# Paired dilated tails, slot sums from the exponentials and wide slot outputs in a windowed attention and soft-MoE kernel

## The chip, the cores and the metric

The kernel runs on one core of one Trainium2 chip. The time is the device time of a run in microseconds; a profile's span, from the first to the last instruction, is some 1.7 us shorter than the time of the same run. A run more than 1.5% above the fastest of its kernel is marked slow. Each group of experiments ran on one chip beside runs of the kernel before on the same chip; the groups used different chips.

Engines are named as in the profile: PE multiplies matrices, PEld loads its weights, DVE and ACT are the vector and scalar engines, POOL is GpSimd, which also issues nearly all transfers, and SP issues the last two. The clock is the share of full speed that PE was granted.

A timeline's line has the start and length in us, the engine, the line of the kernel, what is written and read, for PE the rows and columns of the array that a product uses (`64*128`: 64 rows), the operand's size, how many were merged, and in brackets the idle time before it with what ended it.

## The reference, cut to what matters

```python
def _attn_ref(q, k, v):                       # (8, 8, 576, 64): batch, heads, positions, width
    scores = matmul(q, k.T) / 8
    rel = pos[:, None] - pos[None, :]
    mask_plain = (rel >= 0) & (rel < 32)                       # heads 0 to 3
    mask_dil = (rel >= 0) & (rel < 128) & (rel % 4 == 0)       # heads 4 to 7
    return matmul(softmax(where(mask, scores, -1e9)), v)

def _moe_ref(x, phi, w1, w2):                 # x (4608, 512), 8 experts of 4 slots each
    logits = x @ phi                          # (4608, 32)
    d = softmax of logits over the rows       # slot sums: column sums of exp(logits)
    slot_input = d.T @ x
    slot_out[e] = relu(slot_input[e] @ w1[e]) @ w2[e]
    return softmax(logits over slots) @ slot_out
```

All inputs and the output are fp32 in HBM. The kernel computes in fp16, and the transfers cast.

## The kernel before

A dilated head of 576 positions is four interleaved subsequences of 144 positions: 128 and a tail of 16. In the kernel before each tail is a product of its own, for scores and for values. The attention of a batch and the work that follows it (transposes to x^T, logits, slot sums U) run in a software pipeline over eight batches.

```python
# scores of group 1: two plain tiles, then the four dilated tails
for r in range(DIL):
    w = LEFT if r < 3 else 2 * LEFT                                  # LEFT = 16
    jobs.append((kd, SUB * r + 96, qd, SUB * r + 128, W1 + LEFT * r, w))
...
# values of the tails, one product of 48 x 32 for each head and subsequence
for r in range(DIL):
    c0 = W1 + LEFT * r
    jobs.append((32 * r, 32, n, pt[0:48, h % 2, c0 : c0 + 32], vL[b % NV][0:48, h, r, 0 : D + 1]))
...
# slot sums: a product of ones beside the two products of x for every tile t
jobs.append((4, ones[0:n, :], er[0:n, t, :]))
...
# slot outputs, in two halves of 256 columns
slot_out(0, ORDER[:6]); slot_out(1, ORDER[:6]); slot_out(0, HALVED)   # HALVED = (6, 7)
for pair in range(NSPLIT // 2):
    combine(0, pair)                                                  # first outputs
    ...
```

The weights w2 of experts 6 and 7 arrive last, in two column halves: the first half of the output is computed and written while the second half of these weights is still on its way. The two last pairs of output tiles go out through SP; all other transfers are issued by POOL.

The softmax here doesn't subtract the row's maximum and nothing guards it: scores larger than these inputs give would overflow.

## Time and profile before

| | before |
|---|---|
| time, median of 4 runs | 182.15 us (182.03 to 182.48) |
| span and clock of the profiled run, a fifth one of 182.69 us | 181.0 us, 0.868 |
| PE, DVE, ACT, POOL busy | 81%, 59%, 50%, 46% of the span |
| read, written | 61.93 MB, 9.44 MB: 394 GB/s over the span |
| batch period at full clock (start of the same logits product, 97.32 to 110.99) | 13.67 us |
| first products with w1 | 138.87 us |
| first output issued | 152.88 us |

The batch period counts only where the clock is 1.0 throughout, which it was from 80 to 128 us.

### The profile page before, as it was taken

The numbers are of one execution on the slowest core, as the hardware profiler recorded it, in microseconds if no ns is written. First come the engines' busy times: TensorE is split into PE (matmuls) and PEld (weight loads), VectorE is DVE, ScalarE is ACT, GpSimd is POOL, SyncE is SP. The second block draws the span as 40 slices with busy tenths as digits, with TensorE's granted clock in tenths as the row PEclk, the third lists the DMA queues.
The fourth block names the chain that finished last, engine by engine and source line by source line (L and its number), as shares of the span: only waits on it lengthen the run. The fifth ranks groups of instructions, "written<-read, shape, count | busy, mean of one in ns | idle before, by whom it ended". The sixth has DMA issues, their size and how long they took to land.

```text
span 181.0 us, 5591 instructions
## 1 busy us (share of the span) xinstructions
PE 146.4 (81%) x2464; PEld 87.4 (48%) x2464; DVE 107.5 (59%) x232; ACT 91.0 (50%) x162; POOL 83.9 (46%) x124
## 2 busy tenths in 40 slices
PE   0467977999999999999999999999987986598000
PEld 0133544746755665664674674675735363233000
DVE  4689874875757676588498498453604023389030
ACT  2044454748465484755766776675430024488030
POOL 7953552642623263352544327434410442979900
PEclk9999995798589789789999999999855699879855
DMA  4999999999999999999999999999999999999996
GB/s 60 199 196 208 208 210 214 201 211 214 202 212 214 203 212 214 201 211 213 203 214 211 204 216 210 214 215 215 211 216 213 200 193 163 311 332 409 410 404 239
DMA packets 29527, 40.75 MB, mean 225 GB/s; under 512 B 1856, under 2 KB 19264, under 8 KB 29504
## 3 DMA queue, kind: packets, MB, share of 16 engines
q0 software_dynamic: 28960, 39.36, 116.3%
q1 hardware_dynamic: 544, 1.05, 1.5%
q8 instruction: 19, 0.31, 0.6%
q14 instruction: 4, 0.03, 0.0%
HBM read 61.93 MB, written 9.44 MB: 394 GB/s over the span
## 4 chain that ended last, share of the span: by engine, by line
DMA 43%; PE 34%; ACT 6%; DVE 6%; POOL 5%; issue 3%; POOLq 0%; DVEq 0%
DMA w<-in_moe_w_dram 28%; DMA raw<-in_k_dram 9%; ACT p L293 5%; PE lg L408 5%; PE o_p L339 4%; PE sa L282 4%; DMA out_dram<-ol 4%; PE sb L271 4%; PE sa L271 4%; DMA out_dram<-ot 2%; PE rd L389 2%; DVE qk L245 2%; PE vb L163 2%; PE va L163 2%; PE u L452 2%
## 5 line engine op out<-in xcount | busy, mean ns | idle before, releaser
L293 ACT ACTIVATE p<-sa 128x960 f16<-128x960 f32 (+2 forms) x24 | 21.4, 891 | 33.9 <-PE sb L282 33.4
L339 PEld LDWEIGHTS <-p 128*128 128x128 f16 (+2 forms) x544 | 19.7, 99 | 12.8 <-issue 8.6
L245 DVE STREAM_TRANSPOSE qk<-raw 128x320 uint32<-128x320 uint32 (+1 forms) x32 | 21.6, 678 | 0.3
L271 PE MATMUL sa<-masks,ident 128*128 128x480 f16 (+2 forms) x48 | 15.6, 414 | 7.3 <-POOL masks L489 6.2
L293 ACT ACTIVATE p<-sb 128x960 f16<-128x960 f32 (+2 forms) x24 | 21.2, 884 | 0.0
L236 DVE STREAM_TRANSPOSE qk<-raw 128x576 uint32<-128x576 uint32 x16 | 19.8, 1249 | 0.9 <-DMA raw<-in_q_dram 0.8
L271 PEld LDWEIGHTS <-ident 128*128 128x128 f16 x96 | 9.6, 112 | 18.9 <-issue 7.7
L282 PEld LDWEIGHTS <-qk 32*128 32x128 f16 x832 | 12.6, 100 | 12.0 <-issue 9.8
L408 PE MATMUL lg<-xTd,phi 128*128 128x288 f16 x32 | 18.3, 659 | 0.0
L339 PE MATMUL o_p<-v,p 128*128 128x65 f16 (+1 forms) x288 | 16.6, 202 | 0.8 <-ACT v L172 0.7
L282 PE MATMUL sa<-qk 32*128 32x160 f16 (+4 forms) x416 | 16.5, 217 | 0.8 <-DVE qk L236 0.7
L282 PE MATMUL sb<-qk 32*128 32x160 f16 (+4 forms) x416 | 16.5, 218 | 0.0
L271 PE MATMUL sb<-masks,ident 128*128 128x480 f16 (+2 forms) x48 | 15.4, 411 | 0.5 <-ACT p L293 0.5
L209 POOL COPY v<-v 32x1024 f16<-32x1024 f16 x8 | 8.3, 1036 | 16.1 <-PE sb L282 9.4
L212 POOL DMA_DIRECT2D w<-in_moe_w_dram x16 | 8.9, 554 | 14.4 <-DMA vs<-in_v_dram 6.8
L361 DVE TENSOR_TENSOR xp<-o_p,rc_p 128x448 f16<-128x448 f32 (+1 forms) x24 | 14.4, 602 | 0.8
L361 DVE TENSOR_TENSOR xd<-o_d,rc_d 128x448 f16<-128x448 f32 (+1 forms) x24 | 14.4, 602 | 0.8
L219 POOL DMA_DIRECT2D w<-in_moe_w_dram x10 | 6.7, 673 | 14.5 <-DMA w<-in_moe_w_dram 10.2
L163 PE MATMUL va<-vs,orders 32*128 32x256 f16 (+1 forms) x96 | 12.1, 289 | 1.0 <-ACT p L293 1.0
L412 ACT ACTIVATE ET<-lg 128x288 f16<-128x288 f32 x16 | 6.6, 411 | 12.3 <-PE lg L408 12.1
L360 DVE RECIPROCAL rc_p<-o_p 128x7 f32<-128x7 f32 (+1 forms) x24 | 4.8, 198 | 12.1 <-PE o_p L339 11.6
L382 ACT COPY xTp<-rp 128x576 f16<-128x576 f16 x16 | 10.4, 647 | 2.2 <-PE rp L377 2.2
(108 smaller groups left out, 277.9 us busy)
## 6 DMA issues: line engine op xcount, KB each, us to landing
w<-in_moe_w_dram POOLq DMA_DIRECT2D x16, 512.0 KB, 16.8
w<-in_moe_w_dram POOLq DMA_DIRECT2D x5, 1024.0 KB, 19.3
vs<-in_v_dram POOLq DMA_DIRECT2D x8, 512.0 KB, 14.5
raw<-in_q_dram POOLq DMA_DIRECT2D x7, 576.0 KB, 16.6
raw<-in_k_dram POOLq DMA_DIRECT2D x7, 576.0 KB, 16.8
out_dram<-ot POOLq DMA_DIRECT2D x14, 256.0 KB, 4.2
out_dram<-of POOLq DMA_DIRECT2D x7, 512.0 KB, 4.9
w<-in_moe_w_dram POOLq DMA_DIRECT2D x8, 256.0 KB, 10.2
```

The lines of the kernel that those rows point to most:

```text
L163: nc.tensor.matmul(o.rearrange("p (h d) -> p h d", h=4), l, st[:, 0:4, D * r : D * r + D], start=(r == 0), stop=(r == DIL - 1), skip_group ...
L209: nc.gpsimd.tensor_copy(out=vL[b % NV][0:32, :, :, 0:D], in_=vD[b % NV][96:128, :, :, 0:D])
L212: nc.gpsimd.dma_start(out=w1t[e][:, 2 * i : 2 * i + 2, :].rearrange("p l f -> p (l f)"), in_=moe_w1[e, 256 * i : 256 * i + 256].rearrange( ...
L236: nc.vector.transpose(out=dst, in_=src)
L245: nc.vector.transpose(out=o, in_=i)
L271: nc.tensor.matmul(sps[h // 2][:, h % 2, 0:n], ident, bias[g], start=True, stop=False, skip_group_check=True,)
L282: nc.tensor.matmul(sps[h // 2][:, h % 2, c0 : c0 + w], kt_[32 * h : 32 * h + 32, k0 : k0 + 128, tt], qt_[32 * h : 32 * h + 32, q0 : q0 + w ...
L293: nc.scalar.activation(out=pt, in_=sps[ab][:, :, 0:n], func=AF.Exp, scale=SCALE)
L339: nc.tensor.matmul(o[p0 : p0 + np_, n, :], l, rr, start=(k == 0), stop=(k == len(jobs) - 1), skip_group_check=True,)
L361: nc.vector.tensor_tensor(out=x.rearrange("p t (h d) -> p (t h) d", h=4)[0:nq, u0:u1, :], in0=o[0:nq, 0:n, 0:D], in1=rc[0:nq, 0:n, None].b ...
L382: nc.scalar.copy(out=xTp_t[b][:, c, :], in_=rg)
L408: nc.tensor.matmul(lp, phi4[:, kc].rearrange("p c s -> p (c s)"), rhs, start=(kc == 0), stop=(kc == 3))
```

## The change

Its intent is to take work off PE. The four dilated tails of a head are put in pairs: keys of all four subsequences are gathered into one tile kL by a DVE copy, two products of 64 columns replace four small ones, and the values become two products per head. The slot sums come from the accumulator of ACT's exponential, so the products of ones and the mask of the slot rows go away. The dilated tail's transposes and its products in U use 64 rows and stand next to each other, apart from the 128-row ones; the plain tail's products in U, of 64 rows before, take all 128. The first six experts' slot outputs are computed 512 columns wide, kept aside, and added to the halves of the last two experts on DVE.

```diff
 # scores, group 1
-                for r in range(DIL):
-                    w = LEFT if r < 3 else 2 * LEFT
-                    jobs.append((kd, SUB * r + 96, qd, SUB * r + 128, W1 + LEFT * r, w))
-                n = W1 + NLEFT                                       # 304
+                for u in range(2):
+                    jobs.append((kL[b % 2], 128 * u, None, 0, W1 + NLEFT * u, NLEFT))
+                n = W1 + 2 * NLEFT                                   # 352
...
+                    if qt_ is None:
+                        qq = qd[heads, 0:S, tt].rearrange("p (r i) -> p i r", r=DIL)[:, 128:SUB]
 # values of the tails
-                for r in range(DIL):
-                    ...                                              # 48 x 32, four to a head
+                for u in range(2):
+                    c1 = W1 + NLEFT * (u + 1)
+                    m = (128, 64)[u]
+                    (jobs, over)[u].append(
+                        (128 - m, m, n, pt[:, h % 2, c1 - m : c1], vL[b % NV][:, h, u, 0 : D + 1])
+                    )
 # transposes of the dilated part
-        for r in range(DIL + 1):
+        for r in (0, 1, 2, 3, 4) if c == 0 else (4, 0, 1, 2, 3):
+            p0 = 0 if r < DIL else NLEFT                             # NLEFT = 64
             nc.tensor.transpose(
-                rg[:, 128 * r : 128 * r + 128], xd_t[b][:, r, 128 * c : 128 * c + 128], ident
+                rg[:, 128 * r : 128 * r + 128 - p0],
+                xd_t[b][p0:128, r, 128 * c : 128 * c + 128],
+                ident[p0:128, p0:128],
             )
 # logits and slot sums
-        nc.scalar.activation(out=ET[:, c0 : c0 + n], in_=lp, func=AF.Exp, scale=1.0)
+        nc.scalar.activation(..., accum_out=esum[:, 2 * b + half : 2 * b + half + 1])
...
-            jobs.append((4, ones[0:n, :], er[0:n, t, :]))
 # prologue
+        nc.vector.tensor_scalar(out=masks[:, W1:], in0=masks[:, W1:], scalar1=gap, ..., op0=ALU.max)
 # slot outputs
-        slot_out(0, ORDER[:6])
-        slot_out(1, ORDER[:6])
-        slot_out(0, HALVED)
+        slot_out(so_early, 0, early, True, True)                     # six experts, 512 columns
+        nc.scalar.copy(out=early_sb, in_=so_early)
+        for n in range(2):
+            slot_late(0, n)                                          # then early_sb + so on DVE
```

Cut here: mask building for the pairs (nine selections on POOL instead of five), the layout of vL and kL, the four smaller POOL copies that fill vL, one transpose instead of four in the slot rows, and the small product that spreads the slot sums over the partitions at the end of attention.

## The prediction

> **What bounds the kernel now.** I read the page's rows over 40 slices first, because a kernel with several stages hides behind averages: the summary says PE 81% busy, and that is the wrong thing to believe.
>
> ```profile
> PE   0467977999999999999999999999987986598000
> ...
> DMA  4999999999999999999999999999999999999996
> GB/s 60 199 196 208 208 210 214 201 211 214 202 212 214 203 212 214 201 211 213 203 214 211 204 216 210 214 215 215 211 216 213 200 193 163 311 332 409 410 404 239
> ...
> HBM read 61.93 MB, written 9.44 MB: 394 GB/s over the span
> ```
>
> PE looks full over the middle, but the DMA row is full from the second slice to the last but one, and the moved bytes never fall below about 200 GB/s while inputs load. The loads cast fp32 to fp16, so 61.93 MB read arrive as 30.97 MB. Two stages follow: loads at about 210 GB/s as written (420 GB/s as read), then the output at about 409 GB/s. Estimate of the DMA work alone: 30.97 MB / 209 GB/s = 148 us, plus 9.44 MB / 409 GB/s = 23 us, plus 2.6 us before the first bytes, is 174 of the 181.0 us span.
>
> Next I read the chain that ended last, in order of time, to see whether PE's 15 us per batch or the queue carries the end.
>
> ```profile
> 86.15 16.32 DMA raw<-in_k_dram
> ...
> 102.77 21.17 DMA w<-in_moe_w_dram
> ...
> 125.33 19.26 DMA w<-in_moe_w_dram
> ...
> 146.34 10.34 DMA w<-in_moe_w_dram
> 156.72 0.32 PE so L722 x4
> 157.06 0.38 ACT so_sb L730
> 157.48 2.73 PE f L801 x6
> ```
>
> From 86 us on it is transfers end to end, except for short issues. A load of 512 KB takes 16.8 us from issue to landing (the page's DMA issues), though at 209 GB/s its bytes need 2.5 us: some 14 us of queue stand in front of it. Before 86 us the chain walks through PE because the k load was issued after a DVE transpose, but with 14 us queued a later issue does not leave the DMA engines empty: the bandwidth row shows no hole.
>
> Last the turn from loads to output, from the timeline of PE and the table of windows (columns: stretch, busy of PE, weight loads, DVE, ACT, POOL, clock, DMA share, GB/s).
>
> ```profile
> 138.87 5.82 PE L686 MATMUL hps<-w,siTm 128*32 128x512 f16 x64 [1.06 <-DVE siTm L672]
> ...
> 146.54 3.38 PE L722 MATMUL so<-w,hTm 128*32 128x256 f16 x104 [0.38 <-DVE hTm L703]
> 151.04 0.29 PE L722 MATMUL so<-w,hTm 128*32 128x256 f16 x4 [1.11 <-DMA w<-in_moe_w_dram]
> ```
> ```profile
> 148.00:152.00 4.00, 2.42 (x72) 1.91 (x63) 0.00 (x0) 0.37 (x1) 0.00 (x0) 1.00 1.44 194
> 152.00:154.00 2.00, 1.79 (x20) 1.00 (x18) 1.71 (x4) 1.82 (x5) 1.12 (x3) 1.00 0.83 116
> 154.00:156.00 2.00, 0.97 (x16) 0.50 (x9) 1.26 (x2) 1.06 (x3) 2.00 (x3) 1.00 1.37 254
> ...
> 160.00:162.00 2.00, 1.76 (x8) 0.78 (x7) 1.84 (x4) 1.88 (x5) 1.73 (x3) 0.90 1.03 258
> 162.00:178.00 16.00, 5.25 (x23) 2.11 (x22) 6.67 (x10) 6.13 (x13) 9.55 (x14) 0.77 1.60 407
> ```
>
> The last four slot products of the first half start at 151.04 after 1.11 us of waiting for the w2 load. All PE work before them was done at 149.9, so a faster PE gains nothing here; a slower one has 1.1 us to spare. Only two holes exist: 152 to 154 (116 instead of 194 GB/s, so 2 x (1 - 116/194) = 0.8 us) and 160 to 162 (258 instead of 407, so 0.73 us). Together 1.5 us: all that compute could give back.
>
> **What the skill says.** "DMA: Bandwidth & Descriptors", section Specifications, gives 435 GB/s as the fabric's ceiling and about 358 GB/s for HBM per core. The trace agrees with the first (2 x 212 = 424 as read) and not with the second (394 over the whole span, 409 written). The same page, section "Anatomy of one DMA — SWDGE (gpsimd) path", says that waits happen at the issuing sequencer and that the engines just consume their queues; the 14 us of queue fit. So later or earlier issues don't matter until that queue is drained. "TensorEngine Tiling", section Key Properties, says that changing the tiling mode drains TensorE. That is the change's reason for grouping 64-row products; no row of before separates that cost. "VectorE: DVE Perf Modes", section on the TRN2 errata, gives (N+151)/0.96 ns for an fp32 two-operand add: 424 ns for 256 elements. No 256-element add from PSUM is in this trace; its nearest row, the relu of 256 from PSUM, took 0.43 us.
>
> **The change part by part.** *Attention, per batch at full clock.* Scores of group 1: the mask product grows from 304 to 352 columns, four times; mean starts of 256- and 480-column products suggest 0.4 ns a column, so 4 x 48 x 0.42 = +0.08 us. Of the dilated tails 32 small products, starting over 0.2 us (119.28 to 119.49), become 16 of 64 columns; the eight of 64 columns at 119.22 start over 0.06 us, so 0.12: -0.1. Values: 16 products of 48 rows become 8; the 18 of the last chunk take 0.40 to 0.47 us, about 25 ns each, so 8 x 25 = -0.2. Slot rows: 13 transposes become 10, -0.08. Slot sums: 25 products become 20; 25 took 0.94 to 1.01 us, some 40 ns each with clock losses, so -0.2. PE: **-0.5 us a batch, about -4 us over eight**, before drains saved. ACT: exp of 704 instead of 608 elements, (891-677)/352 = 0.6 to 0.9 ns an element, 2 x 96 x 0.85 = +0.16 us; sums beside the 16 exps of the logits, about +0.1. DVE: the gather of 4 x 48 words about +0.25 us, the masked product of 320 (0.33 us) becomes a plain copy, -0.1. POOL: four copies of 512 elements instead of two of 1024 (1.03 us each), +0.1. All of it is beside the transfers.
>
> *Prologue.* POOL makes nine mask selections instead of five, at about 0.27 us (1.29 us for four): +1.1 us. The new DVE maximum over the masks stands ahead of the first q transpose (6.33 us) and waits for the last selection, at 6.75 + 1.1 = 7.85: the first transposes begin about 1.7 us later. But six loads have been issued by 5.1 us; their 1.73 MB keep the queue busy past 11 us at about 200 GB/s, and the next load moves only from 6.70 to 7.8. Cost to the end: 0.
>
> *Slot sums in the tail of attention.* Reduction, diagonal, one small product and the reciprocal replace one reciprocal (0.29 us): four short steps at 0.15 to 0.3 us, +0.5 to +0.8, partly beside 1.09 us of zero fills. Net for PE before the slot outputs: -4 + 1.7 + 0.6, so 1 to 2 us earlier, into the wait for w2. Gain 0.
>
> *Wide slot outputs.* 96 products of 256 columns become 48 of 512. The stream is the same (104 took 3.38 us, 32 ns each, four side by side); perhaps -0.4 us, again ahead of the wait at 151.04. On the path afterwards a DVE add (about 0.43) stands where an ACT cast (0.37) stood: +0.06 us for each half. The early copy of 512 columns lies in the wait.
>
> *Transfers.* No load or store changes its bytes, its shape or its order. Sum on the path: 0 + 0 + 0 + 0.06 + up to 0.06 = **+0.1 us**, and the PE time saved turns into a longer wait for w2.
>
> **The rivals.** *PE carries the end after all.* The row of nines and the chain before 86 us speak for it; then 4 us less PE would make about 178.5. Against it are the bandwidth row without a hole and PE's wait at 151.04. I give it 1 in 50. *The holes close.* If the clock is full at 158 (it was 0.50 in the window 158 to 160, where six wide products took 2.72 us), the first full-width outputs come 0.4 us earlier and time falls to 181.6; if the throttle lands on the slot outputs instead, 182.8. *The delay comes through.* If prologue and slot sums cost more than thought and PE saves nothing, the slot products end 2.5 us later, overrun the 1.1 us of slack by 1.4 and widen the hole at 152: 183.3 at most. *POOL contention:* smaller copies and waits on DVE delay load issues; harmless while 14 us are queued.
>
> **Range and chances.** Before has a median of 182.14 with runs from 182.03 to 182.48 (the profiled one 182.69), so 0.3% is noise. The prediction is the same time, 182.1 us: +0.1 from the path, and as much back from a PE that stays ahead. Eight in ten: 181.3 to 183.1, from the clock's luck in the holes below and the delay rival above. Faster by over 2% would need 178.5 or less, that is 3.6 us, when the holes hold 1.5: 0.02. Slower by over 2% (above 185.8) would need the queue to run dry during attention: 0.02. Within 2%: 0.96.
>
> **What would show each step.** Right: PE and weight-load busy time fall by several us; loads stay at 200 to 215 GB/s; the last w2 landing stays at 156 to 157; the wait of the slot products for w2 grows from 2.9 us in total. Wrong: a w2 landing that moves by more than 1 us, load bandwidth that differs, or a hole in the DMA row before 150. A later first transpose of about 8 us with no effect at the end would confirm the prologue step. The prediction fails if the queue's bandwidth depends on what the engines do beside it.

## The result, and the profile after

The changed kernel measured 182.41 us (four runs: 182.09, 182.33, 182.49 and a slow one of 184.93) beside 182.15 us before. The ratio is the mean time of one kernel's fast runs over that of the other's in the same rounds, so it is not quite the ratio of these medians: 1.0006, 95% interval 0.9985 to 1.0027.

The profile taken then fell on the slow run. The changed kernel was therefore run twice more (labels again and again_b below), and both of these profiles are of fast runs. The page of the first of them, PE's and the transfers' rows over 40 slices:

```profile
PE   0357886999999999999999999999997888776100
...
DMA  4999999999999999999999999999999999999995
GB/s 65 196 197 207 211 206 215 200 212 212 203 212 215 200 213 216 200 214 211 203 211 216 205 209 216 215 213 212 214 219 210 194 197 157 296 392 408 408 375 215
```

The transfers' row is again full from the second slice to the last but one, at the same 200 to 215 GB/s for the most part; the bytes are the same (61.93 MB read, 9.44 MB written). PE's row is as full as before although it has 2162 products instead of 2464. The slice from 149.6 us shows 157 GB/s where before had 163.

The chain that ended last, in order of time, has one new piece. (The columns are start, length, piece.)

```profile
124.46 19.44 DMA w<-in_moe_w_dram
...
145.64 0.74 POOL w L236
146.38 6.96 issue
153.36 0.53 POOL out_dram L796
```

Before, a transfer of 10.34 us and the last slot products stood in that place; here POOL has issued its last load and waits 6.96 us until the first output is there to be issued. The output comes from PE. So PE's timeline around the turn from loads to output tells more; lines of three profiles of the changed kernel, itself unaltered, follow, first the fast run of again:

```profile
140.95 5.72 PE L728 MATMUL hps<-w,siTm 128*32 128x512 f16 x64 [0.62 <-DVE siTm L714]
...
148.53 2.56 PE L768 MATMUL so_early<-w,hTm 128*32 128x512 f16 x44 [0.38 <-DVE hTm L745]
150.92 0.61 PE L768 MATMUL so<-w,hTm 128*32 128x256 f16 x16
```

then the fast run of again_b:

```profile
137.03 6.32 PE L728 MATMUL hps<-w,siTm 128*32 128x512 f16 x64 [0.62 <-DVE siTm L714]
...
149.62 0.29 PE L768 MATMUL so<-w,hTm 128*32 128x256 f16 x4 [1.05 <-DMA w<-in_moe_w_dram]
```

then the slow run:

```profile
142.51 6.03 PE L728 MATMUL hps<-w,siTm 128*32 128x512 f16 x64 [0.62 <-DVE siTm L714]
```

Before began the products with w1 at 138.87 and waited for w2. The changed kernel begins them at 137.03, 140.95 or 142.51, in three runs of the same program. In the first it waits 1.05 us for w2, as before did; in the second all 16 products of the first half follow each other without a wait, because PE is the later one. In the slow run, too, they follow each other without a wait, and end at 153.4.

What differs between these runs is the clock. Its mean from 12 to 80 us was 0.97 in again_b and 0.92 in again (0.85 before), and from 128 to 148 us 0.74 against 0.57 (0.66 before). The work per batch at full clock is the same in all: 14.12 us in again (82.11 to 96.23) and in again_b (79.82 to 93.94). So a batch became **0.45 us longer**, where the prediction had it 0.5 us shorter, and whether that reached the turn went with the clock. All 16 runs of the changed kernel divide by it: the eight with a clock of 0.902 or less took 182.74 to 184.93 us, the eight with 0.909 or more 181.78 to 182.72. The 33 runs of before beside the experiments, at 0.869 to 0.912, show no such division (181.51 to 183.16). Six of the first eight ran on one chip, and what sets the clock of a run is not shown, so this is two measured things going together and no proof of the cause.

### The profile page after: what moved, and what is told of

The parts are those of the page before. It is cut to its first block, busy times and chain, and to the rows that moved or that the text cites. A ratio compares the mean times of both kernels' runs of the same rounds, so it can differ in the third digit from the quotient of the medians.

```text
span 183.2 us, 5048 instructions
## 1 busy us (share of the span) xinstructions
PE 147.7 (81%) x2162; PEld 85.3 (47%) x2162; DVE 111.0 (61%) x253; ACT 93.2 (51%) x177; POOL 87.3 (48%) x144
## 3 DMA queue, kind: packets, MB, share of 16 engines
q1 hardware_dynamic: 544, 1.05, 1.5%
HBM read 61.93 MB, written 9.44 MB: 390 GB/s over the span
## 4 chain that ended last, share of the span: by engine, by line
DMA 36%; PE 34%; issue 10%; ACT 7%; POOL 6%; DVE 3%; POOLq 0%; DVEq 0%; ACTq 0%
DMA w<-in_moe_w_dram 22%; DMA raw<-in_k_dram 8%; PE sa L302 6%; PE o_p L354 5%; ACT p L313 5%; PE lg L426 5%; DMA out_dram<-ol 4%; PE sb L286 4%; PE sa L286 4%; DMA out_dram<-of 2%; PE rd L405 2%; PE vb L167 2%; PE va L167 2%; POOL out_dram L834 1%; POOL raw L142 1%
## 5 line engine op out<-in xcount | busy, mean ns | idle before, releaser
L313 ACT ACTIVATE p<-sa 128x960 f16<-128x960 f32 (+2 forms) x24 | 22.0, 917 | 36.2 <-PE sb L302 36.2
L354 PEld LDWEIGHTS <-p 128*128 128x128 f16 (+2 forms) x480 | 21.4, 103 | 14.0 <-issue 9.8
L313 ACT ACTIVATE p<-sb 128x960 f16<-128x960 f32 (+2 forms) x24 | 21.9, 912 | 0.0
L216 POOL COPY v<-v 32x512 f16<-32x512 f16 x16 | 9.7, 609 | 22.5 <-DVE v L206 22.0
L354 PE MATMUL o_p<-v,p 128*128 128x65 f16 (+1 forms) x288 | 17.1, 206 | 0.7 <-ACT v L176 0.7
L302 PEld LDWEIGHTS <-qk 32*128 32x128 f16 x576 | 10.5, 102 | 13.5 <-issue 10.0
L302 PE MATMUL sa<-qk 32*128 32x160 f16 (+2 forms) x288 | 14.7, 240 | 2.2 <-DVE qk L245 2.2
L302 PE MATMUL sb<-qk 32*128 32x160 f16 (+2 forms) x288 | 14.7, 240 | 0.0
```

Of the source, the lines that this page charges most:

```text
L216: nc.gpsimd.tensor_copy(out=vL[b % NV][64 * w : 64 * w + 32, :, :, 0:D], in_=high[:, :, :, w, 0:D])
L302: nc.tensor.matmul(sps[h // 2][:, h % 2, c0 : c0 + w], kt_[heads, k0 : k0 + 128, tt], qq, start=False, stop=(jn == len(jobs) - 1 and tt == 1),
L313: nc.scalar.activation(out=pt, in_=sps[ab][:, :, 0:n], func=AF.Exp, scale=SCALE)
L354: nc.tensor.matmul(o[p0 : p0 + np_, n, :], l, rr, start=(k == 0), stop=(k == len(jobs) - 1), skip_group_check=True,)
```

## Where a batch's time went

The steady batch around 90 us, at full clock in both, can be cut at the same products. PE's timeline of before:

```profile
89.41 0.47 PE L339 MATMUL o_d<-v,p 128*128 128x65 f16 x18
89.81 0.53 PE L377 MATMUL rp<-ident,xp 128*128 128x128 f16 x5
...
90.57 0.18 PE L452 MATMUL u<-er,ones 128*128 128x32 f16 x1
90.68 0.21 PE L452 MATMUL u<-er,xp 64*128 64x32 f16 x2
...
90.85 0.42 PE L452 MATMUL u<-er,xd 128*128 128x32 f16 x10
91.11 0.42 PE L271 MATMUL sa<-masks,ident 128*128 128x304 f16 x2
...
92.27 0.58 PE L339 MATMUL o_p<-v,p 128*128 128x65 f16 x10
92.79 0.73 PE L389 MATMUL rd<-ident,xd 128*128 128x128 f16 x10
93.36 0.59 PE L271 MATMUL sa<-masks,ident 128*128 128x512 f16 x2
```

and of the changed kernel (again):

```profile
89.67 0.60 PE L354 MATMUL o_d<-v,p 128*128 128x65 f16 x10
90.20 0.53 PE L392 MATMUL rp<-ident,xp 128*128 128x128 f16 x5
...
91.35 0.47 PE L286 MATMUL sa<-masks,ident 128*128 128x352 f16 x2
...
92.28 0.27 PE L302 MATMUL sa<-qk,v 32*128 32x64 f16 x2
...
92.81 0.58 PE L354 MATMUL o_p<-v,p 128*128 128x65 f16 x10
93.33 0.89 PE L405 MATMUL rd<-ident,xd 128*128 128x128 f16 x10
94.06 0.59 PE L286 MATMUL sa<-masks,ident 128*128 128x512 f16 x2
```

Ends of PE products are modelled, so the table takes differences of starts. The slot sums begin at 90.28 before and at 90.66 in again; the other starts not shown above (slot rows and the wait for the exponentials) are read in the same timelines.

| stretch of a batch | before | changed | predicted difference | measured |
|---|---|---|---|---|
| last values of the dilated part, with the tails | 0.40 | 0.53 | -0.2 | +0.13 |
| slot sums | 0.83 | 0.69 | -0.2 | -0.14 |
| scores of group 1 with their mask products | 1.16 | 1.46 | 0 | +0.30 |
| ten transposes of the dilated part | 0.57 | 0.73 | not priced | +0.16 |
| transposes of the slot rows | 0.49 | 0.38 | -0.08 | -0.11 |
| from one ordering product of v to the next, a wait for ACT | 0.50 | 0.61 | not priced | +0.11 |
| sum | | | -0.5 | +0.45 |

What the slot rows saved came back at once as a longer wait for the exponentials: the same exponential of ACT ends that stretch in both.

The timeline of before already holds the price of a change of shape. In the slot sums, products of one shape start 0.025 us apart; the first of 64 rows starts 0.11 us after the last of 128 (90.57 to 90.68), the third of them starts 0.026 us after the second, and the first of 128 again 0.105 us after the third. So here it is the change of shape that costs, not the 64 rows. Of the three places concerned, before makes such a visit to another shape and back in the slot sums and in the tail values, but none in the transposes; the changed kernel makes one in each.

## The experiments

Twelve experiments were made. In the table, the ratio is to the fast runs of before on the same chip. "First output" and "end of data" are the start of the first output bytes and the end of the last bytes in the trace's records of transfers, in us from the span's start, in the profiled run. The 184.93 us run is in it for its turn only.

| label | what it is | time, us | ratio (95% interval) | first output | end of data |
|---|---|---|---|---|---|
| (before) | | 182.15 | | 154.00 | 179.61 |
| (changed, slow run) | | 184.93 | | 156.35 | 181.97 |
| again | changed kernel | 182.88 | 1.0048 (1.0026 to 1.0070) | 154.48 | 180.01 |
| again_b | changed kernel, other chip | 182.09 | 1.0011 (0.9976 to 1.0046) | 152.75 | 179.01 |
| full128 | changed, nothing at 64 rows | 182.12 | 1.0004 (0.9983 to 1.0025) | 152.68 | 179.11 |
| sums_wide | before with two of the parts | 181.93 | 0.9990 (0.9970 to 1.0011) | 153.67 | 178.79 |
| plain_q | changed, queries read side by side | 181.97 | one run | 152.63 | 179.04 |
| less_load | before, one load less | 179.50 | 0.9859 (0.9827 to 0.9891) | 150.78 | 176.13 |
| full128_less | full128, one load less | 179.65 | 0.9859 (0.9823 to 0.9895) | 150.34 | 176.76 |
| more_pe | before, more PE work in attention | 182.06 | 0.9995 (0.9962 to 1.0027) | 153.84 | 179.37 |
| late_hps | before, more PE work after attention | 182.24 | 0.9993 (0.9968 to 1.0019) | 154.77 | 179.60 |
| max_later | changed, prologue reordered | 182.38 | 1.0013 (0.9974 to 1.0052) | 156.51 (slow run) | 182.52 |
| own_last | full128, own buffers for the last pairs | 184.79 | 1.0147 (1.0112 to 1.0182) | 152.95 | 179.25 |
| one_halved | full128, one expert in halves | 183.82 | 1.0091 (1.0072 to 1.0110) | 155.63 | 181.37 |

### The changed kernel again (again, again_b)

No edit.

> The changed kernel unchanged, for its ordinary state: the one profile of it fell on a run of 184.93 us beside three of 182.09 to 182.49. Theory (the transfer queue sets the end, and compute only matters where it comes later than the last w2 loads): a fast run shows the same batch period of 14.1 us at full clock as the slow one, against 13.67 before, but its slot products end by about 151 to 152 us, and the hole after 152 us is not much deeper than before (116 GB/s), unlike 15 GB/s in 154 to 156 of the slow run. Rival (the slow run was slow in its transfers): loads would land later in the slow run than in this one. Time 182.0 to 182.6, about one run in four 1 to 3 us longer.

> The changed kernel once more, as the control for these runs on the same chip: 182.3 to 183.0, first output issued at 153 to 153.5 us; if its clock is better than 0.90, at 152.5 and time as before.

Measured: 182.88 us (182.74 to 183.97) on one chip, 0.5% slower than before and clear of its interval; 182.09 us (181.78 to 183.85) on another, no difference. The first is above the 182.0 to 182.6 that was expected. The period of 14.12 us came out as expected. In again the slot products ended at about 151.5, after the load instead of before it. The windows of two microseconds show what that does (the last column is GB/s), again:

```profile
154.00:156.00 2.00, 1.38 (x22) 0.64 (x20) 1.85 (x4) 1.49 (x4) 2.00 (x4) 1.00 1.01 197
```

again_b:

```profile
154.00:156.00 2.00, 0.51 (x5) 0.21 (x5) 0.46 (x2) 0.00 (x0) 2.00 (x4) 1.00 1.87 374
...
174.00:176.00 2.00, 0.00 (x0) 0.00 (x0) 1.22 (x2) 1.05 (x2) 0.00 (x0) 0.50 1.03 251
```

and the slow run:

```profile
154.00:156.00 2.00, 1.76 (x16) 1.10 (x19) 1.53 (x4) 1.52 (x4) 0.78 (x2) 1.00 0.10 15
```

Where the slot products of the first half end at 149.9 us, that window has 374 GB/s, where they end at 151.5 it has 197, and at 153.4 it has 15. Loads do not explain it: their last bytes came at 154.52 in the slow run, at 154.70 and at 154.64 in the fast ones. So the rival, that the slow run was slow in its transfers, falls. What the traces show in its place is a late first output, with the end moved by about the same amount: from again to the slow run the first output is 1.87 us later and the end of data 1.96.

In all, the changed kernel, unaltered, made 16 runs, three of them above 183.8 us (183.85, 183.97, 184.93). Before made 37 beside the changed kernel and the experiments, none above 183.16.

### What the 64-row products cost (full128)

```diff
-                    m = (128, 64)[u]
-                    (jobs, over)[u].append(
+                    m = 128
+                    jobs.append(
...
+                rg[:, 128 * r : 128 * r + 128], xd_t[b][:, r, 128 * c : 128 * c + 128], ident
...
+        nc.vector.memset(er[0:NLEFT, NT + DIL, :], 0.0)
-            p0 = 0 if r < DIL else NLEFT
+            p0 = 0
```

> The changed kernel with everything of 64 rows or 64 columns at full height instead: the paired tail products all 128 x 128 in the first group, the transposes 128 rows, the slot sums 128 rows with rows 0 to 63 of the slot row zeroed. Still a right result. Theory A (changing the array's tile size costs, and grouping does not remove it): the three segments of a batch that grew or hardly shrank give back about 0.14 (tail values), 0.16 (transposes) and 0.08 us (slot sums), period at full clock 14.12 falls to about 13.75. Theory B (these products are dear for another reason): period stays at 14.1. Time: the same within 0.5% either way, 181.7 to 182.6, since the queue sets the end.

Measured: the period at full clock fell from 14.12 to 13.58 us (91.36 to 104.94), more than theory A asked. PE's timeline of this variant:

```profile
85.33 0.48 PE L354 MATMUL o_d<-v,p 128*128 128x65 f16 x10
85.65 0.52 PE L392 MATMUL rp<-ident,xp 128*128 128x128 f16 x5
...
88.58 0.73 PE L404 MATMUL rd<-ident,xd 128*128 128x128 f16 x10
89.15 0.59 PE L286 MATMUL sa<-masks,ident 128*128 128x512 f16 x2
```

The tail values take 0.32 us instead of 0.53, the transposes 0.57 instead of 0.73, and the slot sums 0.52 instead of 0.69. Twice the rows, or columns, cost nothing; one visit to a shape of 64 rows or columns and back costs 0.16 to 0.21 us. The single records of again put the time at the changes themselves, as in the slot sums of before: among the transposes the 64-row ones start 0.15 us after a full one, and a full one 0.12 us after them, against 0.056 between full ones. That speaks for theory A and against B. The grouping that the change makes leaves one such visit in each of the three places, and that is still more than the small products save. The time came back to that of before (1.0004), but not below it.

### What the gathered queries cost (plain_q)

```diff
-                        qq = qd[heads, 0:S, tt].rearrange("p (r i) -> p i r", r=DIL)[:, 128:SUB]
+                        qq = qd[heads, 128 : 128 + NLEFT, tt]
```

> The changed kernel with the moving operand of the paired tail scores read as 64 neighbouring columns instead of four groups gathered across the subsequences (wrong result on purpose; 16 products a batch keep their shape). In the slow profile the segment from the mask products of group 1 to the first value product took 1.46 us against 1.16 before, of which the 48 added mask columns explain about 0.1. If the strided read is what makes the paired scores dear, this segment falls to about 1.25; if not (16 products of 64 columns simply take that long, or the wait is for the exponentials), it stays at 1.4 to 1.5.

The queries are wrong here on purpose. The comparison with the reference does not prove this part right in any version. PE's timeline:

```profile
90.93 0.19 PE L302 MATMUL sa<-qk,v 32*128 32x64 f16 x2
...
91.14 0.58 PE L354 MATMUL o_p<-v,p 128*128 128x65 f16 x10
```

The 16 paired products take 0.21 us from first start to the next work, against 0.53 us (92.28 to 92.81) in the changed kernel; in before the 32 small ones took 0.33 (91.94 to 92.27). So pairing would have saved 0.12 us, and reading 64 queries across four subsequences, 576 bytes from one to the next, costs 0.32. The Trainium skill, page "SBUF — State Buffer", in its note on cache lines under "Door 1: The DMA port swizzle", says that full bandwidth needs at least two accesses to a line of 16 bytes. That fits: neighbouring queries of one half are 4 bytes apart, four to a line, the gathered ones have a line each. That the lines are the reason, and not the two-step pattern of addresses, is not shown: plain_q changes both. The page does not give a cost for PE; this case's is 2.5 times.

### Two parts alone (sums_wide)

Before, with the accumulator of the exponential in place of the products of ones, and with the wide slot outputs. The edits are those of the change's diff for these two parts; the mask of the slot rows stays.

> The kernel before with two parts of the change alone: slot sums from ACT and wide slot outputs, no paired tails, no 64-row groups. Theory: the five products of ones per batch go (about 0.14 us), period at full clock 13.67 falls to about 13.5; no added prologue; PE reaches the slot outputs 1 to 2 us earlier than before and waits longer for w2, total of that wait 3.5 to 5 us instead of 2.9. Time 181.6 to 182.3: nothing gained beyond what closes of the hole at 152. Rival (PE sets the end): time falls by 1.5 us or more.

Measured: period 13.54 us (81.80 to 95.34), 0.13 below before, as expected. PE did not reach the slot outputs earlier (products with w1 at 139.00 against 138.87): the half-clock stretch near the end began at 126.4 instead of 129.7 in the profiled run. The total wait for w2 was 2.4 us, not 3.5 to 5. The time is that of before, 0.9990. The rival that PE sets the end fails here by itself, but the test is weak, since PE's start of the slot work hardly moved.

### One load less (less_load, full128_less)

```diff
     def load_w1(e, i):
+        if (e, i) == (3, 1):
+            nc.vector.memset(w1t[e][:, 2 * i : 2 * i + 2, :], 0.0)
+            return
```

> The kernel before with one of the 16 loads of w1 left out (1.05 MB of 61.93 MB read; its half tile is filled with zeros instead, so the result is wrong on purpose). At 2 x 209 GB/s the queue is 2.5 us shorter. Theory (queue bound, with 1.1 us of slack for PE): the last load of the first half would land near 148.5, but PE ends the work before it at about 149.9, so only some 1.1 us of the 2.5 come through and the hole after 152 grows: 180.8 to 181.3 us, wait of the slot products for w2 well below 2.9 us. Rival 1 (queue alone): 179.6. Rival 2 (PE alone): 182.1.

> The same load left out of the full-height variant of the changed kernel, whose PE reaches the slot outputs about 5 us earlier than that of before (products with w1 begin at 133.9 instead of 138.9 us). Theory: here PE keeps ahead even of a shorter queue, so the whole 2.5 us come through: 179.4 to 180.0. If PE were what sets the end of both, it would gain no more than the kernel before does with the same load left out.

The results are wrong, as meant (relative error 0.24). Measured: 179.50 us from before and 179.65 from full128, the same ratio 0.9859. Both gain 2.5 to 2.6 us for 1.05 MB, 403 GB/s for 2.6 us: the pace of the queue. The expectation that PE's slack of 1.1 us would cap the first was wrong. In that profile PE began the products with w1 at 134.80, 4 us earlier than in the profile of before, with a better clock (0.902 against 0.868), and it waited 2.3 us for w2. So the slack of 1.1 us that was read from one profile is one draw of a quantity that moves by several microseconds.

### More PE work (more_pe, late_hps)

```diff
-        for h in range(4):
+        for h in (0, 1, 2, 3) * (2 if g == 1 else 1):      # more_pe: mask products of group 1 twice
...
-    for fc in range(2):
+    for fc in (0, 1, 1):                                   # late_hps: second half of the w1 products twice
```

> The kernel before with the mask products of score group 1 made twice (four products of 304 columns, about 0.5 us a batch at full clock, 4 us in all; right result). Theory: attention ends about 4 us later; less the 1.1 us of slack the first outputs come 2.5 to 3 us later, the hole at 152 to 156 falls to some 15 GB/s as in the slow run of the changed kernel, time 184.0 to 185.0. That would show that the slow run needs no slow state of the chip, only a late PE. Rival (PE time is wholly hidden): 182.2.

> The kernel before with the second half of the w1 products made twice (32 more products, 2.9 us at half clock, 1.45 at full; right result). The earlier attempt to make PE late put the work into attention, where the granted clock rose and ate it: only 1.8 us arrived at the w1 products. Here it stands directly before the slot outputs. Theory (the end follows the first output when PE is later than the last load of the first half): first output bytes 2 us later than the 154.0 us of before, so 183.2 to 184.3 us, with a deep hole in 152 to 156. Rival (the slowest transfer engine sets the end and the hole of the others is free): 182.1.

Both expectations failed: 182.06 and 182.24 us, no difference from before. In more_pe the period rose by a whole microsecond, from 13.67 to 14.68 (82.40 to 97.08), which should be 8 us over eight batches, yet the w1 products began only 1.8 us later (140.66), because the clock was at half for 6.8 us near the end instead of 13.6, and for less of the first 80 us. In late_hps the profiled run reached the w1 products at 134.41, so its 32 more products ended before the loads, and PE still waited 1.78 us for the last one. What they show is the other side: PE in before can have a microsecond more per batch without any loss. That the end follows the first output once PE is late is read from the three profiles of the changed kernel and from one_halved below, not from these two.

These two and three other profiles without the paired tails show what holds the end when PE is not late. In before, sums_wide, less_load, more_pe and late_hps alike the last bytes of the loads and the end of data lie 23.28 us apart, to 0.01 us (before: 156.33 and 179.61), although the first output starts anywhere from 1.55 to 2.33 us before the loads end.

### The prologue (max_later)

```diff
-        nc.vector.tensor_scalar(out=masks[:, W1:], in0=masks[:, W1:], scalar1=gap, ..., op0=ALU.max)
         qk_plain(0, 0)
         qk_plain(1, 0)
         nc.vector.memset(ones32, 1.0)
+        nc.vector.tensor_scalar(out=masks[:, W1:], in0=masks[:, W1:], scalar1=gap, ..., op0=ALU.max)
```

> The changed kernel with the new maximum over the tail masks moved behind the first two q and k transposes, so that these start at about 6.3 us again instead of 7.76. Nothing else. The batch period stays at 14.1 us. Theory: attention ends about 1.3 us earlier than in the changed kernel beside it, PE reaches the slot outputs before the load or with it, and the 0.5% that the changed kernel lost on this chip come back: 182.0 to 182.5. Rival (the loss came from something else in the change, in the output stage): 182.9 as before.

Inconclusive. The q transpose began at 6.26 again, but the k transpose then waited for its load until 8.72, and the dilated transposes began at 11.41 instead of 11.18: there was nothing to be had from the order. The control on that chip was not slower than before either, so there was no loss to bring back. Two of its six runs were 184.20 and 185.47 us; the profile fell on the latter, a slow one, with the same half-clock stretches as the first slow run up to the output.

### Own buffers for the last outputs (own_last)

```diff
-            tag = "last0" if pair == NFIN // 2 - 2 else "last1"
-            ot = out_pool.tile([128, 2, DMODEL], FP32, name=f"ol_{pair}", tag=tag)
+            else:
+                ot = w1t[pair - NFIN // 2 + 2].rearrange("p l f -> p (l f)")[:, 0 : 4 * DMODEL]
+                ot = ot.bitcast(FP32).rearrange("p (k n) -> p k n", k=2)
```

> The full-height variant with the last two output pairs in the dead tiles of w1 instead of the two buffers that earlier outputs hold. In its own profile the hole at 152 is closed (193 GB/s) but another stands at 174 to 176 (216 instead of 408 GB/s, worth 0.9 us): ACT and DVE wait 7.8 and 7.4 us for the landing of an earlier output before they may write the last pair. Theory: what came in front was lost to that buffer wait, so own buffers give 0.5 to 0.9 us: 181.2 to 181.7, and no such hole. Rival (the slowest of the 16 transfer engines sets the end and holes of the mean are not on its path): time stays at 182.1 though the hole is gone.

The reason for it, in the waits of full128:

```profile
ACT ol L851 <- DMA out_dram<-last_a: 7.8, 1, 7.8
```

In own_last that wait is gone and the window from 174 to 176 is full:

```profile
174.00:176.00 2.00, 0.00 (x0) 0.00 (x0) 0.00 (x0) 0.00 (x0) 0.00 (x0) 0.50 1.92 399
```

but the kernel is 1.5% slower, and neither theory had that. The records of the transfers and of POOL's closing drain, the last instruction that POOL ends before all engines meet, say why (us from the span's start):

```
            last bytes of POOL's queue   of SP's queue   POOL's drain ends   span
before              177.04                  179.61            179.78         181.0
full128             176.54                  179.11            179.20         180.4
own_last            179.25                  177.27            181.86         182.6
```

The last bytes of all come at 179.11 with the wait and at 179.25 without it, as the rival had it. But POOL's drain ends 2.6 to 2.75 us after the last bytes of POOL's own queue, in all three. Before and full128 send the last megabyte through SP while POOL drains, so that the drain is hidden; own_last sent it early, POOL's queue became the last one, and the drain was added. The old buffers, which were taken for a flaw, keep the last pair behind the others, and that order is worth more than the hole. In the last 1.1 us of POOL's queue in own_last 27 packets of 1 KB start some 40 ns apart, one by one, which reads like a single transfer engine behind the others. Which one, and why, the trace does not say.

### One expert in halves (one_halved)

```diff
-    HALVED = (6, 7)
-    ORDER = (1, 4, 2, 3, 5, 0) + HALVED
+    HALVED = (7,)
+    ORDER = (1, 4, 2, 3, 5, 0, 6) + HALVED
```

> An attempt at a version that beats both: the full-height variant with only one expert's w2 loaded in halves (expert 6 whole, so 1 MB moves at 213 instead of 196 GB/s). Gain in the loads 0.4 us. Cost: only 0.5 MB (2.6 us) of loads are left behind the landing that starts the outputs, and the turn from landing to first output bytes took about 3 us, so a hole of 0.4 us may open. 181.6 to 182.3: probably nothing.

Slower, 1.0091. That is outside what was expected. With expert 6 whole, the wide products wait 4.22 us for it; the first output starts at 155.63, 2.9 us later than in full128, and the data end 2.3 us later. The two halves are doing their work. No version was found that beats both kernels by more than the noise; sums_wide, at 0.9990, is the best of the right ones and not told apart from before.

## Why the prediction was right, and where not

**The time**: 182.1 predicted, 182.41 measured, within 181.3 to 183.1. The view on which it rests was right too, as long as PE is not late. The transfers set the end: a load less brings its own 2.5 to 2.6 us whichever kernel it is taken from, while more_pe and full128, with periods of 14.68 and 13.58 us and the products with w1 at 140.66 and 133.89, take the same time. That the changed kernel stayed so close is in part luck: the time was forecast with a PE that comes earlier, and it held because a PE that needed more time met a better clock in half of its runs.

**PE's saving of 0.5 us a batch** was the step that failed. It is +0.45 us. Three terms of the sum were wrong. "Scores of group 1" priced the pairs as 16 neighbouring reads of 64 columns, 0.12 us, and they took 0.53, of which 0.32 is the gathered read. "Values" took 25 ns for each product removed, but in the single records of before the sixteen start within 0.11 us (89.58 to 89.69), and 0.25 us of their stretch are the two changes of shape around them. The eight new ones keep two such changes, to 128 x 64 and back; full128, without them, takes 0.21 us less. "Before drains saved" expected a saving where the transposes, until then all of 128 rows, got a visit to another shape to pay: +0.16; the slot sums have one before and after. That "no row of before separates that cost" was a misreading: its slot sums do (90.57 to 90.85). Only the products of ones and the transposes of the slot rows came out near their size, and the latter was lost to a wait for ACT. The 0.1 us on DVE did not come either: product and copy took 317 ns each.

**The prologue** was put at 1.7 us later for the first transpose; it is 7.77 instead of 6.33, so 1.4, and the dilated ones 1.0 (11.18 instead of 10.17), part of which the k load would have taken anyway. It costs the end nothing that could be seen.

**The slot sums in the tail of attention** were put at +0.5 to +0.8 us. From the start of the last slot-sum products of x to the products with w1 it is 2.56 us before (136.31 to 138.87) and 2.65 in again (138.30 to 140.95), so +0.1: the steps lie beside the row sums that PE makes at that moment.

**Net for PE, 1 to 2 us earlier,** was wrong in sign at full clock. Since the extra 0.45 us a batch makes 3.6 us over eight, the changed kernel should come well after the load; that it does so only sometimes goes with the granted clock, which was better in its fast runs (0.88 to 0.93) than in the profile of before (0.868; other runs of before had 0.87 to 0.91). The prediction's "wait for w2 grows from 2.9 us" was false in again (0.4 us, and that for the early product) and about right in again_b (2.7). Its sign that the busy time of PE and of the weight loads falls by several us came out in again_b (146.4 to 143.0, 87.4 to 82.6), for PE hardly in again (145.5); but busy time holds the clock, too.

**The rival "the delay comes through"** had the right mechanism: slot products that overrun the load widen the hole and move the end. It was given a PE that "saves nothing" and at most 183.3 us, where its own sum, an overrun of 1.4 us on 182.1, makes 183.5. It is what the slow run shows at 184.93 and what again shows at 182.88.

**The two holes, "all that compute could give back"**, gave nothing. In full128 and again_b the one at 152 to 154 is closed (193 and 182 GB/s instead of 116), and the time is the same; a new hole stands at 174 to 176, and taking that away too does not move the last bytes. After 152 us in before, 573 of the 4,096 packets of the halved loads had not ended, 74 of them not at 155: the hole looks like the tail of transfer engines that are behind, while the others have run out. The mean over 16 engines hid that. That the hindmost engine sets the end is argued from this, from the 23.28 us that five profiles share and from the last packets of own_last; it is not shown engine by engine.

**The last w2 landing** was to stay at 156 to 157 us. Its last bytes come at 156.33 before and at 154.5 to 154.7 in the changed kernel, a shift of over 1 us, which the prediction had named as a sign of being wrong. It belongs to the paired tails: all the full-load profiles with them end their loads at 154.5 to 155.3, those without at 155.5 to 156.3. Nevertheless the output gains little: from the last load to the last bytes of POOL's queue it takes 20.7 us in all five profiles without them, and 21.8 in again_b. Why the loads end earlier and what the output loses is open.

**The citations.** The 435 GB/s that the prediction cites is a figure for the side of SBUF, where the loads bring 212 GB/s; the 424 set beside it are bytes as read from HBM, so that agreement tests little. The cited formula for an add gave an estimate of 424 ns; the two adds took 416 ns on average in again, against 0.37 us for the cast.

## What to carry to other kernels

Where the transfers are always behind, a saving elsewhere moves a wait, and the quickest proof is to leave a load out and see whether the time falls by its bytes. Slack read from one profile is one draw: between runs of the same program, with different granted clocks, PE came up to 5 us earlier or later, so a change that eats slack shows first as a few long runs, not in the median. Small products are cheap to count and hard to price: look at the shape changes they bring and at the spacing of what they read before the number of instructions.

## What the Trainium skill lacked or had wrong

- "TensorEngine Tiling", Key Properties, says that a change of mode drains the array, without a size. Here the first slot-sum product after a change started 0.11 us after the one before it, against 0.025 within a shape, and one visit to 64-row or 64-column products among full ones cost 0.16 (transposes), 0.17 (slot sums) and 0.21 us (values) a batch, more than the halved products saved.
- No page says what a widely spaced moving operand costs a product: 16 products of 32 rows by 64 columns took 0.53 us with elements 576 bytes apart and 0.21 us with elements 4 bytes apart.
- "ScalarE: Activation LUTs", What it computes, says that an activation can give an accumulator output, but not that it is a further instruction: the trace has 16 ACTIVATION_READ_ACCUMULATOR of 194 ns each.
- "VectorE: DVE Perf Modes", The perf-mode tier table, gives a product of two operands with one in PSUM 1×, and a copy from PSUM at most 2×. Here the product of 320 fp16 elements, one operand in PSUM, took 317 ns, the same as the copy that replaced it; fp32 products from PSUM took 321 ns for 160 elements and 624 for 448, on whose line 320 would take about 490 (an estimate). So the table's 1× does not hold for this 16-bit product.
- "DMA: Bandwidth & Descriptors" has no word of POOL's closing drain: it ended 2.6 to 2.75 us after the last bytes of POOL's own queue in before, full128 and own_last, hidden where SP's queue wrote last; own_last, where POOL's was the last, was 1.5% slower.
- The same page's Specifications give about 358 GB/s per core for HBM; this core moved 394 over the whole span. "HBM Reference", Specifications, says itself that a core alone measures more.
